# A chunked recurrence in front of two feed-forward layers: one triangular inverse for the first four chunks, and a new start

## The chip, the cores and the metric

The kernel runs on one core of a Trainium2 chip. The metric is the device time of one execution in microseconds (us); three runs of the kernel before gave 1090.04, 1091.82 and 1099.68 us, and their median, 1091.82 us, is the time before. The engines are TensorE (PE in the profile, with its weight loads as PEld), VectorE (DVE), ScalarE (ACT), GpSimd (POOL) and SyncE (SP, which only issues DMA transfers here).

## The reference

An attention-like recurrence over 768 steps for 4 batches of 8 heads with a state of 40 x 40, then two feed-forward layers over the 3072 tokens. All of it is float32.

```python
state = zeros((B, H, D, D))                       # B, H, S, D = 4, 8, 768, 40
for t in range(S):
    y[:, :, t] = einsum('bhd,bhde->bhe', rt, state)
    Sa = einsum('bhde,bhe->bhd', state, at)
    state = state * wt[:, :, None, :] - einsum('bhd,bhe->bhde', Sa, bt)
    state = state + einsum('bhd,bhe->bhde', vt, kt)
x = y.transpose(0, 2, 1, 3).reshape(3072, 320)
h = x @ w_in;   x = (h * tanh(log1p(exp(h)))) @ w_out      # 320 -> 2048 -> 320 (mish; h itself above 20)
h = x @ w_in2;  out = (h * cos(h)) @ w_out2
```

## The kernel before

**The recurrence** is cut in time into 24 chunks of 32 tokens and in batches into two halves of 16 heads, which gives 48 chunk steps, `g` = 0 to 47 (chunk `g // 2`, half `g % 2`). Every chunk step has work that doesn't need the state, `pre(g)` and `inverse`, and work that does, `chain(g)`.

`pre(g)` loads a, k, b and w (tile IN; for step 1 a part of TMP). VectorE scans the decays into PE (L570) and their inverse into RP (L575, L576), scales a into AM (L584, two passes) and k and b into KB (L590, two passes); GpSimd clears the other rows of AM (L598). TensorE multiplies AM by KB (L607, 8 matmuls), VectorE masks the product into AM (L617, four instructions of 64 partitions and 128 elements). Two DMAs store a triangular part to DRAM (`l_d`, L630, L631). TensorE transposes KB (L640), and ScalarE copies that into FL (L390).

`inverse(bt)` inverts the unit triangular 32 x 32 matrices of a batch of two chunk steps. They are read back into XM, one matrix half in a partition (L667, 64 partitions), 14 columns are worked off by a multiplication (L682, into XT) and an addition (L680), on VectorE for the batches 0 to 2 and on GpSimd for the others; the result goes to DRAM (`t_d`, L693) and back (TT, L697). `halves` joins the two halves with a transposition on VectorE and matmuls (L719, L721).

`chain(g)` runs from the state of step `g - 2`: right-hand sides (L790) to RS (L796), the multiplication by TT (L804, L813), copies into FR and VR, a product (L862) and its masked eviction (L872, 64 x 256), the matmul for the outputs and the new state (L888), evictions to SV (L899) and Y (L907), a transposition of the state (L932). After every second chunk Y is stored to `x_d`.

**The first layer** takes 256 tokens at a time (12 blocks). A block loads XR from `x_d` (L1042 to L1044), splits it into a high part XH (L1047) and a low part XL (L1049), and runs 8 rounds of matmuls (L991), Mish on ScalarE, GL on VectorE (L1067) and output matmuls (L972). Its weights come as pairs of 32-bit words and are converted in `prep`: load (L454), L461 on ScalarE, L466, L471 and L479 on VectorE, a high part (L390 or L392) and a low part on GpSimd (L508). The late half of w_out passes through two small buffers, RL. The second layer follows the same way and is not touched.

**The order on each engine** is fixed before the kernel runs. Every piece of work is a `Task` with an engine, a cost, predecessors, buffers (rings) and a priority; the class `Plan` goes through all tasks with these costs and writes one list for each engine, SP's transfers among them. Priorities come from a base and the step: -1e4 for `chain`, -5e3 for `pre`, -4921 for the weights, 0 and up for the layers. Lines that matter here:

```python
BATCH = [(i, 2) for i in range(0, TOT, 2)]
own = bt >= 3
ldma[g] = P.add("SP", 1.0, ldm, preds=t_gl, lat=DMA_LAT, prio=pr)
t_k = fifo("kb", P.add(*am_on(g, 0.65), kb_f(0), preds=[t_rp], acq=[("KB", k("KB"))], prio=pr, port=True))
t_b = P.add(*am_on(g, 0.65), kb_f(1), preds=[t_k, t_a1], ...)
```

Of the kernel before, what the change touches and what calls it, by code (L numbers as in the profile page):

```python
# [18 lines left out]
D = 40  # L19
# [69 lines left out]
SP_SAFE = 1.0  # L89

# [8 lines left out]
class Plan:  # L99
# [23 lines left out]
    def run(self):  # L123
# [12 lines left out]
        port_free = 0.0  # L136
# [4 lines left out]
        while done < len(self.tasks):  # L141
# [88 lines left out]
            t.end = free[e] + (0.2 if t.lat is None else t.lat)  # L230
# [6 lines left out]
            for u in t.succ:  # L237
                for x in u.engs:
                    u.ready[x] = max(u.ready[x], free[e] + (HOP.get((e, x), 0.15) if t.lat is None else t.lat))
# [12 lines left out]
def body(ctx, tc, ins, out):  # L252
# [11 lines left out]
    BATCH = [(i, 2) for i in range(0, TOT, 2)]  # L264
# [46 lines left out]
    P.ring("XR", 1), P.ring("XH", 2), P.ring("XL", 2), P.ring("OB", 2)  # L311

    D1 = at.tile([104, NQ, C + 1], F32, name="D1")
    IN_t = [at.tile([104, 3 * 256 + 265], F32, name=f"IN{i}") for i in range(N_IN)]
    IN1 = TMP[0:104, 4096:4096 + 1033]
# [20 lines left out]
    for n, k in (("IN", N_IN), ("PE", LA), ("AM", LA), ("FL", LA), ("RP", 1), ("KB", 1), ("SV", N_SV),  # L336
                 ("FR", N_FR), ("VR", N_VR), ("X", N_X), ("TT", N_TT), ("RS", 2), ("ZS", 1), ("Y", N_Y),
                 ("PA", 4), ("PH", 2), ("PO", 2)):
# [67 lines left out]
    DMA_LAT = 3.0  # L406
# [6 lines left out]
    AHEAD_W = 6  # L413
# [3 lines left out]
    am_on, GLE = lambda g, d: ("DVE", 0.385), ("DVE",)  # L417
# [4 lines left out]
    W1_AFTER = lambda: None  # L422
    W2_PRIO = 5e3
# [8 lines left out]
    def prep(layer, names, prio, after, stage, stage2, half):  # L432
# [7 lines left out]
        for (kind, k, cc), h, n in parts:  # L440
            late = kind == "out" and cc >= 5
            if late and t_sw is None:
# [12 lines left out]
                       preds=after + ([t_sw] if late else []) + loads[-AHEAD_W:][:1] * (len(loads) >= AHEAD_W),  # L455
                       acq=[(rring, (key, "r"))], lat=DMA_LAT + 1.5, prio=prio)
# [85 lines left out]
    Gev, KBe, scanT, ldma, ttld, tt_last, ytask = {}, {}, {}, {}, {}, {}, {}  # L542
    io, Sev, STev, chain_last = {}, {}, {}, {}
# [9 lines left out]
    def pre(g):  # L553
# [5 lines left out]
        pe, am, kb, rp = (lambda: PE_t[P.at(k("PE"))]), (lambda: AM_t[P.at(k("AM"))]), \  # L559
# [794 lines left out]
```

## Time and profile before

| what | value |
|---|---|
| runs of the kernel before | 1090.04, 1091.82, 1099.68 us |
| the profiled execution: its time, its span | 1096.53 us, 1094.8 us |
| instructions in the span | 36345 |
| busy over the span: TensorE, VectorE | 1011.0 us (92%), 746.4 us (68%) |
| busy over the span: ScalarE, GpSimd | 544.2 us (50%), 439.7 us (40%) |
| mean granted TensorE clock | 0.989 |

Busy time is the time in which an engine worked on an instruction. The span runs from the first to the last record of the profiled execution; its own time holds 1.7 us more. A busy share over the whole span says little here, because the first 130 us and the rest have different limits, and the views that matter are those of stretches.

### The profile page before, as it was taken

The numbers are of one execution on the slowest core, as the hardware profiler recorded it, in microseconds if no ns is written. First come the engines' busy times: TensorE is split into PE (matmuls) and PEld (weight loads), VectorE is DVE, ScalarE is ACT, GpSimd is POOL, SyncE is SP. The second block draws the span as 40 slices with busy tenths as digits, with TensorE's granted clock in tenths as the row PEclk, the third lists the DMA queues.
The fourth block names the chain that finished last, engine by engine and source line by source line (L and its number), as shares of the span: only waits on it lengthen the run. The fifth ranks groups of instructions, "written<-read, shape, count | busy, mean of one in ns | idle before, by whom it ended". The sixth has DMA issues, their size and how long they took to land.

```text
span 1094.8 us, 36345 instructions
## 1 busy us (share of the span) xinstructions
PE 1011.0 (92%) x14888; PEld 928.6 (85%) x14888; DVE 746.4 (68%) x1667; ACT 544.2 (50%) x1342; POOL 439.7 (40%) x885
## 2 busy tenths in 40 slices
PE   2266899899999999999999999999999999999998
PEld 1256798798988898988899989999999999999997
DVE  8999887768677677667743797446655556565555
ACT  3255666655565565655665544444433434343433
POOL 5215367553464655444730233103333333333332
PEclk9999899999999999989999999999999999999999
DMA  8555564646555565555543543211100202010100
GB/s 243 147 152 159 158 181 128 167 118 187 135 130 155 133 164 133 136 136 153 139 106 87 174 146 104 71 46 45 42 13 1 54 1 53 1 40 1 25 1 25
DMA packets 109366, 111.88 MB, mean 102 GB/s; under 512 B 64144, under 2 KB 88720, under 8 KB 109200
## 3 DMA queue, kind: packets, MB, share of 16 engines
q1 hardware_dynamic: 108880, 109.24, 36.6%
q8 instruction: 117, 1.92, 0.7%
q14 instruction: 49, 0.40, 0.1%
q10 hardware_dynamic: 320, 0.33, 0.1%
HBM read 91.43 MB, written 18.09 MB: 100 GB/s over the span
## 4 chain that ended last, share of the span: by engine, by line
PE 73%; DVE 11%; DMA 5%; issue 4%; POOL 3%; ACT 3%; SPq 1%; DVEq 0%; POOLq 0%; ACTq 0%
PE bank L991 16%; PE bank L972 15%; PE bank L1006 13%; PE bank L1022 13%; PE bank L888 4%; PE bank L862 2%; PE bank L836 2%; PE bank L607 2%; PE bank L640 1%; POOL XT L682 1%; PE bank L804 1%; DMA TT<-t_d 1%; DMA XM<-l_d 1%; PE bank L790 1%; PE bank L932 1%
## 5 line engine op out<-in xcount | busy, mean ns | idle before, releaser
L1150 POOL TENSOR_TENSOR GL<-H,GH 128x512 fp32r<-128x512 f32 x94 | 121.9, 1297 | 235.7 <-ACT GH L1148 219.1
L682 POOL TENSOR_TENSOR XT<-XM 64x14 f32<-64x14 f32 (+6 forms) x294 | 106.8, 363 | 180.8 <-DMA XM<-l_d 150.9
L390 ACT ACTIVATE FL<-bank 64x160 f32<-64x160 f32 (+1 forms) x376 | 101.5, 295 | 92.5 <-PE bank L932 45.4
L1141 ACT ACTIVATE T<-T,half_pi 128x512 f32<-128x512 f32 x96 | 69.4, 723 | 105.3 <-DVE T L1138 105.3
L1134 DVE TENSOR_SCALAR T<-bank 128x512 f32<-128x512 f32 x96 | 66.4, 692 | 76.6 <-PE bank L1006 63.0
L1067 DVE TENSOR_TENSOR GL<-H,GH 128x512 fp32r<-128x512 f32 x96 | 70.7, 739 | 69.7 <-ACT GH L1064 69.0
L680 POOL TENSOR_TENSOR XM<-XM,XT 64x14 f32<-64x14 f32 (+6 forms) x294 | 107.3, 365 | 22.5
L1062 ACT ACTIVATE H<-bank 128x512 f32<-128x512 f32 x96 | 57.5, 598 | 105.7 <-PE bank L991 105.0
L1143 DVE TENSOR_TENSOR H<-bank,T 128x512 f32<-128x512 f32 x96 | 66.1, 689 | 54.0 <-ACT T L1141 53.2
L1148 ACT ACTIVATE GH<-H 128x512 fp32r<-128x512 f32 x96 | 60.6, 632 | 73.9 <-DVE H L1143 72.7
L991 PE MATMUL bank<-XH,wih 128*128 128x256 f32 x448 | 94.9, 294 | 0.2 <-ACT GH L1064 0.2
L991 PE MATMUL bank<-XH,wil 128*128 128x256 f32 x448 | 90.0, 283 | 0.0
L991 PE MATMUL bank<-XL,wih 128*128 128x256 f32 x448 | 89.7, 282 | 0.0
L607 PE MATMUL bank<-AM,KB 104*64 104x64 f32 x768 | 37.3, 248 | 49.9 <-DVE KB L590 41.6
L617 DVE TENSOR_TENSOR AM<-bank,maskG 64x128 f32<-64x128 f32 x192 | 55.2, 287 | 34.8 <-PE bank L607 22.6
L607 PEld LDWEIGHTS bank<-AM,KB 104*64 104x64 f32 x768 | 30.9, 157 | 54.6 <-issue 38.6
L991 PEld LDWEIGHTS bank<-XH,wih 128*128 128x128 f32 x448 | 70.5, 193 | 2.2 <-ACT GH L1064 0.4
L991 PEld LDWEIGHTS bank<-XL,wih 128*128 128x128 f32 x448 | 69.7, 192 | 1.4 <-issue 1.4
L991 PEld LDWEIGHTS bank<-XH,wil 128*128 128x128 f32 x448 | 69.8, 193 | 0.0
L991 PE MATMUL bank<-XH,wix 128*128 128x256 f32 x224 | 67.8, 302 | 1.3 <-issue 1.3
L1138 DVE SCALAR_TENSOR_TENSOR T<-T,bank 128x512 f32<-128x512 f32 x96 | 65.7, 685 | 2.4
L888 PE MATMUL bank<-FR,FL 104*64 104x72 f32 x1536 | 62.9, 239 | 2.6 <-ACT wih L390 1.7
(173 smaller groups left out, 2933.4 us busy)
## 6 DMA issues: line engine op xcount, KB each, us to landing
VR<-in_vR_dram SPq DMA_DIRECT2D x96, 160.0 KB
IN<-in_inT_dram SPq DMA_DIRECT2D x94, 161.4 KB
FR<-in_rI_dram SPq DMA_DIRECT2D x48, 180.0 KB
FR<-in_vF_dram SPq DMA_DIRECT2D x48, 144.0 KB
TMP<-in_w_in_dram SPq DMA_DIRECT2D x12, 512.0 KB
RA<-in_w_in_dram SPq DMA_DIRECT2D x12, 512.0 KB
RA<-in_w_out_dram SPq DMA_DIRECT2D x10, 512.0 KB
SV<-in_vS_dram SPq DMA_DIRECT2D x96, 52.0 KB
```

What stands on the lines that cost most here:

```text
L390: A.activation(o, i, AF.Copy)
L607: PE.matmul(gp[c0:c0 + 64, q // 2], kb()[:, q].rearrange("p a t -> p (a t)"), am()[0:104, :, q], start=True, stop=True)
L680: IE.tensor_tensor(out=b[:, 0:i, i + 1:16], in0=b[:, 0:i, i + 1:16], in1=tv, op=ALU.add)
L682: IE.tensor_tensor(out=tv, in0=bc(b[:, i:i + 1, i + 1:16], (2 * n, i, w)), in1=bc(b[:, 0:i, i:i + 1], (2 * n, i, w)), op=ALU.mult)
L888: PE.matmul(fp[64 * p:64 * p + 64, qp], fl()[0:104, n * D:n * D + 64], fr()[:, n], start=True, stop=True)
L972: PE.matmul(o, l[:, f, tsl], r, start=(first and f == 0 and i == 0), stop=(last and f == 1 and i == 2))
L991: PE.matmul(hp[:, f], pss[i][0], pss[i][1], start=(i == 0), stop=(i == 7))
L1006: PE.matmul(bank[P.at((key, "h"))][:, 0:512], pss[i][0], pss[i][1], start=(i == 0), stop=(i == 7))
L1022: PE.matmul(o, l, r, start=(ft == 0 and i == 0), stop=(ft == NFF - 1 and i == 2))
L1067: gl = P.add(GLE, (dve(512),), lambda eng, Hv=Hv, key=key: EN[eng].tensor_tensor(out=GL_t[P.at((key, "gl"))], in0=Hv(), in1=GH_t[P.at((key ...
L1141: c = P.add("ACT", act(512, False, 1), lambda f=f, Tv=Tv: A.activation(Tv(f), Tv(f), AF.Sin, scale=-TWO_PI, bias=half_pi), preds=[b], aset ...
L1150: gl = P.add(*((VG, (pool(512), dve(512))) if final and quad == 7 else ("POOL", pool(512))), lambda eng, f=f, Hv=Hv, key=key: EN[eng].tens ...
```

## The change

- `BATCH` begins with one batch of four chunk steps (128 partitions of XM); the others keep two. VectorE inverts the batches 0 and 1 (`OWN`), that is the steps 0 to 5 as before, in two inversions where there were three.
- The transfers of batch 0 (`l_d`, XM, `t_d`, TT; `QUICK`) are issued on ScalarE's queue.
- k and b are scaled by one instruction (`kb_f`, 104 x 512).
- For the first 14 steps (`SPLIT`) the chunk product is 16 matmuls that read only the 40 rows in use; GpSimd clears nothing, and VectorE evicts in two instructions of 64 x 256.
- Clearing of SV, VR, `half_pi` and of the first states in FL goes from VectorE to GpSimd.
- The input tiles are cleared and loaded in the order 0, 2, 1, ahead of the weights; the weight loads are gated on input loads and on the load of TT. All eight PSUM banks serve the recurrence until XR of block 0 is loaded. Step 7 keeps its PE in an output buffer. For chunk 1, Y is evicted ahead of SV, and block 0's input gets a chain priority.
- `Plan` computes when a transfer lands from its size and a queue, no longer as a constant.

```diff
-    BATCH = [(i, 2) for i in range(0, TOT, 2)]
+    BATCH = [(0, 4)] + [(i, 2) for i in range(4, TOT, 2)]
...
     def setup_v():
         for t in SV_t:
-            V.memset(t, 0.0)
+            G.memset(t, 0.0)
         for t in VR_t:
-            V.memset(t[32:64], 0.0)
-        V.memset(half_pi, math.pi / 2)
+            G.memset(t[32:64], 0.0)
+        G.memset(half_pi, math.pi / 2)
...
+    OWN = 2
+    SPLIT = 14
+    QUICK = 4
+    AHEAD_W = 5
+    W1_FREE = 4
...
-                       preds=after + ([t_sw] if late else []) + loads[-AHEAD_W:][:1] * (len(loads) >= AHEAD_W),
-                       acq=[(rring, (key, "r"))], lat=DMA_LAT + 1.5, prio=prio)
+                       preds=(after if layer == 2 else [tt_ld[2]] if len(loads) >= W1_FREE else [t_in[2]]) + ([t_sw] if late else []) + (loads[-AHEAD_W:][:1] * (len(loads) >= AHEAD_W) if len(loads) >= W1_FREE else loads[-1:]),
+                       acq=[(rring, (key, "r"))], kb=0.5 * n, prio=prio)
...
-        def kb_f(j):
-            return lambda eng: EN[eng].tensor_tensor(out=kb()[:, :, j], in0=sl(1 + j), in1=rp()[:, :, 1:], op=ALU.mult)
+        def kb_f(eng):
+            EN[eng].tensor_tensor(
+                out=kb().rearrange("p q j t -> p j q t"), in0=INv()[:, 256:768].rearrange("p (j q t) -> p j q t", j=2, t=C),
+                in1=bc(rp()[:, :, 1:].unsqueeze(1), (104, 2, NQ, C)), op=ALU.mult)
...
+        split = g < SPLIT
+        if not split:
+            t_z0 = P.add("POOL", 0.31, az_f(0), preds=[t_a1], prio=pr)
+            t_z1 = P.add("POOL", 0.31, az_f(1), preds=[t_z0], prio=pr)
...
             for q in range(NQ):
+                if split:
+                    for p in range(2):
+                        r, o = slice(64 * p, 64 * p + 40), slice(64 - 64 * p, 128 - 64 * p)
+                        PE.matmul(gp[o, q], kb()[r, q].rearrange("p a t -> p (a t)"), am()[r, p, q], start=True, stop=True)
+                    continue
...
+                if split:
+                    V.tensor_tensor(out=am()[r, p], in0=pa(k("G"))[r, 0:256].rearrange("r (q t) -> r q t", t=C),
+                                    in1=bc(maskG[r].unsqueeze(1), (64, NQ, C)), op=ALU.mult)
+                    return
...
+        quick = g < QUICK
+        Q = A if quick else SP
         def ldm():
-            SP.dma_start(ld_v[ci, 0], am()[96:128, 0])
-            SP.dma_start(ld_v[ci, 1], am()[32:64, 1])
+            Q.dma_start(ld_v[ci, 0], am()[96:128, 0])
+            Q.dma_start(ld_v[ci, 1], am()[32:64, 1])
...
-        own = bt >= 3
+        own = bt >= OWN
...
+        early = c == 1
...
+            if early:
+                yevs.append(P.add("DVE", 0.26, yev(h), preds=[ft] + yevs, acq=y_acq, prio=pr - 30))
...
+        prx = -9.955e3 if blk == 0 else pr0
...
-            V.memset(FL_t[P.at(("FL", g))][64:104, 0:NU * D], 0.0)
+            G.memset(FL_t[P.at(("FL", g))][64:104, 0:NU * D], 0.0)
```

On ScalarE, at its very start, the queue of the kernel before begins with the weights' first pass (H from TMP) and its copies, and holds no transfer (FL0 is step 0's transposed KB, RS its right-hand sides).

```order
L461 ACT_TABLE_LOAD
L461 ACTIVATE H0_177<-TMP_172 128x512
L461 ACTIVATE H1_178<-TMP_172 128x512
L461 ACTIVATE H2_179<-TMP_172 128x512
L390 ACTIVATE wih1_164<-H0_177 128x512
L390 ACTIVATE wih1_164<-H1_178 128x512
L390 ACTIVATE wix1_166<-H2_179 64x512
L390 ACTIVATE GH0_180<-H2_179 64x512
L390 ACTIVATE FL0_208<-bank1_145 64x160 x4
```

In the changed kernel the same queue, from where step 3 has been transposed, holds the stores of `l_d`, the load of XM, the store of `t_d` and both loads of TT, with weights between them.

```order
L662 DMA l_d0_93<-AM3_202 32x8x32
L663 DMA l_d0_93<-AM3_202 32x8x32
L396 ACTIVATE FL3_209<-bank1_143 64x160 x4
L471 ACTIVATE H1_176<-TMP_170 128x512
L706 DMA XM_222<-l_d0_93 64x512 x2
L396 ACTIVATE wih1_162<-H1_176 128x512
L471 ACTIVATE H2_177<-TMP_170 128x512
L471 ACTIVATE H0_175<-TMP_170 128x512
L734 DMA t_d0_116<-XM_222 64x512 x2
L740 DMA TT0_229<-t_d0_116 128x8x32
L740 DMA TT1_230<-t_d0_116 128x8x32
```

Two weights' passes now stand in front of the store of `t_d`, and the weights' copies wait behind the transfers. On VectorE, in front of the first inversion, the kernel before evicts step 2 (AM2), works on weights and scales k and b of step 3 in two passes; the first inversion's first step is the last row.

```order
L584 TENSOR_TENSOR AM3_204<-IN0_192,PE3_197 40x256
L617 TENSOR_TENSOR AM2_203<-bank1_145,maskG_175 64x4x32 x4
L471 SCALAR_TENSOR_TENSOR H1_178<-TMP_172,H1_178 128x512
L590 TENSOR_TENSOR KB0_217<-IN0_192,RP0_215 104x8x32
L466 TENSOR_SCALAR H2_179<-H2_179 128x512
L590 TENSOR_TENSOR KB0_217<-IN0_192,RP0_215 104x8x32
L682 TENSOR_TENSOR XT_225<-XM_224 64x14
```

In the changed kernel it scales k and b of step 3 in one pass, evicts step 3 right behind it, and has seven instructions between that eviction and the first step, of 128 partitions.

```order
L605 TENSOR_TENSOR KB0_215<-IN0_190,RP0_213 104x2x8x32
L642 TENSOR_TENSOR AM3_202<-bank0_142,maskG_173 64x256 x2
L476 TENSOR_SCALAR H1_176<-H1_176 128x512
L481 SCALAR_TENSOR_TENSOR H1_176<-TMP_170,H1_176 128x512
L583 SCALAR_TENSOR_TENSOR PE4_196<-IN1_191,D1_189 104x264
L590 RECIPROCAL D1R_214<-PE4_196 104x8
L591 SCALAR_TENSOR_TENSOR RP0_213<-IN1_191,D1R_214 104x264
L599 TENSOR_TENSOR AM4_203<-IN1_191,PE4_196 40x256
L723 TENSOR_TENSOR XT_223<-XM_222 128x14
```

The eviction of step 3, its transfers and the inversion stand closer together, with a PE product and two DMA trips between. On TensorE, where block 1 of the first layer begins (XH1), the kernel before comes from block 0's matmuls, with one transposition of the chain (L836) just ahead.

```order
L991 MATMUL bank5_149<-XL0_187,wih1_164 128x256 x2
L991 MATMUL bank5_149<-XL0_187,wix1_166 128x256
L836 MATMUL bank1_145<-ident_173,ZS0_230 40x128 x4
L991 MATMUL bank4_148<-XH1_186,wih1_164 128x256 x2
L991 MATMUL bank4_148<-XH1_186,wil1_165 128x256 x2
```

In the changed kernel a state transposition (L984), the products L908 and L632 and `halves` (L764) stand just ahead of the same row; counted over the whole queue up to it, there are the products of twelve steps (L908) where there were eight (L862), the output and state matmuls and the state transpositions (L984) of eleven steps where there were eight (L888, L932), and the right-hand sides of twelve where there were ten (L790).

```order
L984 MATMUL bank2_144<-ident_171,SV0_216 104x40 x4
L984 MATMUL bank0_142<-ident_171,SV0_216 104x40 x4
L908 MATMUL bank6_148<-VR1_221 64x64 x8
L632 MATMUL bank3_145<-AM1_200,KB0_215 64x64 x8
L764 MATMUL bank2_144<-TA_224,TT0_229 32x32 x32
L1043 MATMUL bank4_146<-XH1_184,wih1_162 128x256 x2
```

More of the recurrence's work lies ahead of block 1 than before.

## Rows read from the trace of the kernel before

**Rows 1.** Windows: busy time (count) of PE, PEld, DVE, ACT, POOL; clock; DMA share; GB/s.

```profile
0.00:131.20 131.20, 67.73 (x1700) 56.84 (x1700) 120.22 (x331) 59.44 (x164) 47.36 (x107) 0.98 0.63 178
131.20:167.90 36.70, 36.49 (x562) 34.13 (x562) 31.15 (x84) 23.33 (x64) 22.92 (x53) 0.94 0.53 146
220.00:600.00 380.00, 370.79 (x8382) 335.92 (x8381) 259.27 (x692) 219.91 (x659) 180.18 (x522) 0.98 0.52 136
```

**Rows 2.** Waits of TensorE, 0 to 132 us: total us, times, longest.

```profile
PE bank L607 <- DVE KB L590: 41.6, 6, 16.9
```

**Rows 3.** Timeline of VectorE: start, us, line, operation; in brackets the idle time before.

```profile
16.39 0.42 DVE L590 TENSOR_TENSOR KB<-IN,RP 104x256 f32<-104x256 f32 x1
16.72 0.76 DVE L466 TENSOR_SCALAR H<-H 128x512 uint32<-128x512 uint32 x2
17.39 1.29 DVE L471 SCALAR_TENSOR_TENSOR H<-TMP,H 128x512 uint32<-128x512 uint32 x2
18.71 1.25 DVE L617 TENSOR_TENSOR AM<-bank,maskG 64x128 f32<-64x128 f32 x4
19.88 0.69 DVE L570 TENSOR_TENSOR_SCAN PE<-TMP,D 104x264 f32<-104x264 f32 x1
...
37.34 1.07 DVE L682 TENSOR_TENSOR XT<-XM 64x14 f32<-64x14 f32 x1 [0.28 <-DMA XM<-l_d]
...
130.24 0.96 DVE L1049 TENSOR_TENSOR XL<-XR,XH 128x768 fp32r<-128x768 f32 x1
...
166.91 0.95 DVE L1049 TENSOR_TENSOR XL<-XR,XH 128x768 fp32r<-128x768 f32 x1
```

**Rows 4.** Timeline of TensorE: the first matmuls of blocks 0 and 1.

```profile
132.45 0.80 PE L991 MATMUL bank<-XH,wih 128*128 128x256 f32 x2
...
174.03 0.48 PE L991 MATMUL bank<-XH,wih 128*128 128x256 f32 x2
```

**Rows 5.** VectorE by line and shape, 0 to 160 us: busy, mean ns | idle.

```profile
L617 DVE TENSOR_TENSOR AM<-bank,maskG 64x128 f32<-64x128 f32 x52 | 15.0, 288 | 2.8 <-PE bank L607 1.7
L872 DVE TENSOR_TENSOR FR<-bank,maskR 64x256 f32<-64x256 f32 x16 | 6.5, 418 | 1.4 <-PE bank L862 0.9 <-ACT FR L390 0.3
L355 DVE MEMSET VR<- 32x1024 f32 x2 | 1.8, 912 | 0.4 <-issue 0.4
L353 DVE MEMSET SV<- 128x832 f32 x2 | 1.5, 752 | 0.2
L682 DVE TENSOR_TENSOR XT<-XM 64x56 f32<-64x56 f32 x6 | 1.2, 204 | 0.1
L1206 DVE MEMSET FL<- 40x640 f32 x2 | 1.2, 592 | 0.4 <-issue 0.4
```

**Rows 6.** Timeline of GpSimd, its first weight pass.

```profile
17.29 4.36 POOL L508 TENSOR_TENSOR wil<-H,wih 128x512 fp32r<-128x512 f32 x2 [9.01 <-ACT wih L390]
```

**Rows 7.** The chain that ended last: start, us, what.

```profile
29.83 3.57 DMA l_d<-AM
...
87.37 2.10 DMA l_d<-AM
```

**Rows 8.** TensorE by line, 220 to 560 us: busy, mean ns | idle.

```profile
L888 PE MATMUL bank<-FR,FL 104*64 104x72 f32 x962 | 36.1, 229 | 0.1
L862 PE MATMUL bank<-VR 104*64 104x64 f32 x496 | 18.3, 225 | 0.0
L932 PE MATMUL bank<-ident,SV 40*104 40x40 f32 x240 | 16.4, 224 | 0.6 <-DVE Y L907 0.2
L790 PE MATMUL bank<-SV,AM 96*32 96x40 f32 (+1 forms) x960 | 13.1, 205 | 0.7 <-issue 0.4 <-DVE Y L907 0.3
```

**Rows 9.** Tile RL, all its instructions: ns min/median/max, first and last start.

```profile
L454 SPq DMA_DIRECT2D RL<-in_w_out_dram x10: 351/372/519, 124.1 to 179.2; - x10
...
L508 POOL TENSOR_TENSOR wol1b<-RL,woh1b x10: 716/733/2134, 145.4 to 189.8; 128x256 fp32r<-128x256 f32 x10
```

**Rows 10.** Windows, TensorE: busy time (count), clock, DMA share, GB/s.

```profile
125.00:130.00 5.00, 3.50 (x156) 0.54 0.85 212
```

More of the change, by code (lines that the diff above doesn't have):

```diff
@@ L135, in run @@
         done = 0
-        port_free = 0.0
+        port_free, queue = 0.0, 1.5
         recent = []
@@ L229, in run @@
                 port_free = free[e]
-            t.end = free[e] + (0.2 if t.lat is None else t.lat)
+            lat = t.lat
+            if t.kb:
+                queue = max(queue, free[e]) + t.kb / RATE
+                lat = queue + LAND - free[e]
+            t.end = free[e] + (0.2 if lat is None else lat)
             for key in t.rel:
@@ L621, in pre @@
         t_gl = []
-        for c2 in range(2):
+        for c2 in range(1 if split else 2):
             for p in range(2):
-                t_gl.append(P.add("DVE", 0.27, gev(p, c2), preds=[t_g], rel=[k("G")], prio=pr))
+                t_gl.append(P.add("DVE", 0.4 if split else 0.27, gev(p, c2), preds=[t_g], rel=[k("G")], prio=pr))
         Gev[g] = t_gl
@@ L657, in inverse @@
         n = cnt * NU
-        rows = lambda: slice(64 * P.at(("X", bt)), 64 * P.at(("X", bt)) + 2 * n)
+        slots = [("X", bt, i) for i in range((cnt + 1) // 2)]
+        r0 = lambda: 64 * min(P.at(i) for i in slots)
+        rows = lambda: slice(r0(), r0() + 2 * n)
         x = lambda: XM[rows(), 0:528]
@@ L915, in chain @@
         sevs, yevs = [], []
+        early = c == 1
         for h, ft in ((0, f0), (1, f1)):
             s = []
-            if not last:
+            rel = [k(f"F{h}")] + ([k("PE")] if h == 1 and g != PX else [])
+            y_acq = [("Y", ykey)] if (yc == 0 and h == 0) else []
+            if early:
+                yevs.append(P.add("DVE", 0.26, yev(h), preds=[ft] + yevs, acq=y_acq, prio=pr - 30))
+                for p in range(2):
+                    s.append(P.add("DVE", 0.315, sev(h, p), preds=[yevs[-1], io[nx][2]] + s, rel=rel if p else [], prio=pr))
+            elif not last:
                 s = [P.add("DVE", 0.315, sev(h, p), preds=[ft, io[nx][2]], prio=pr) for p in range(2)]
             sevs += s
-            rel = [k(f"F{h}")] + ([k("PE")] if h == 1 else [])
-            y_acq = [("Y", ykey)] if (yc == 0 and h == 0) else []
-            yevs.append(P.add("DVE", 0.26, yev(h), preds=[ft] + s + yevs, acq=y_acq, rel=rel, prio=pr + 1))
+            if not early:
+                yevs.append(P.add("DVE", 0.26, yev(h), preds=[ft] + s + yevs, acq=y_acq, rel=rel, prio=pr + 1))
         Sev[g] = sevs
@@ L1188, in body @@
     state_init = {}
+    for g in range(4):
+        pre(g)
+    inverse(0)
     for g in range(TOT):
+        if g > 3:
+            pre(g)
         load_step(g)
-        pre(g)
-        if BT_OF[g][1] == BATCH[BT_OF[g][0]][1] - 1:
+        if g > 3 and BT_OF[g][1] == BATCH[BT_OF[g][0]][1] - 1:
             inverse(BT_OF[g][0])
@@ L1233, in switch @@
             P.grow(r, range(len(STG[r])), P.time)
-        P.grow("PH", [0, 1], P.time)
-        P.grow("PO", [2, 3], P.time)
+        rest = sorted(i for _, i in P.rings["PA"])
+        P.grow("PH", rest[0:2], P.time)
+        P.grow("PO", rest[2:4], P.time)
     def half2():
```

122 lines of the change are left out of this document (70 added, 52 removed).

## The prediction

> **What bounds the kernel now.** I read the windows first [rows 1]. Up to 131.2 us VectorE works 120.22 us (91.6%) and TensorE 67.73. Then it turns: from 131.2 to 167.9 TensorE is busy 36.49 of 36.70 us, and between 220 and 600 us 370.79 of 380. So VectorE sets the end of the first stretch, and TensorE everything behind it. The waits say the same: of TensorE's idle time up to 132 us, 41.6 us end with the scaling of k and b on VectorE [rows 2]. From this follows how the change can pay: TensorE's work behind 132 us is fixed, and the end comes earlier by the work of TensorE that is done earlier, that is by the time at which VectorE lets it through. Two marks show this: the low part of block 0's input is written at 130.24 us and that of block 1 at 166.91 [rows 3], and their first matmuls run at 132.45 and 174.03 [rows 4].
>
> **Part by part**, for the stretch up to block 1's input, on VectorE.
>
> *Clearing.* Two VR at 0.912 us, two SV at 0.752 and two FL at 0.592 go to GpSimd [rows 5]: 4.5 us. GpSimd sat idle for 9.01 us ahead of its first weight pass at 17.29 [rows 6], so it costs nothing there. If the masks, which stand first, left no room, the first use of SV would wait at most the 4.5 us that were saved.
>
> *One inversion less.* 28 instructions at about 0.20 us (the 64x56 form of [rows 5], the largest): 5.6 us. The inversion that is left has 128 partitions where there were 64. Rows suggest that the time goes by the elements in a partition and not by the partitions: 256 elements take 0.42 us in 104 partitions (L590, [rows 3]) and 0.418 in 64 (L872, [rows 5]). So I take the price of a step as unchanged; the other bound, double, is a rival below.
>
> *Chunk products.* Four evictions of 0.288 us become two of 64x256, for which L872 with the same shape has 0.418 [rows 5]: 1.15 to 0.84, or 0.31 us a step, for 14 steps 4.4 us. On TensorE 16 matmuls with 40 rows take the place of 8; it waits in this stretch, and I put it at nothing. GpSimd's clearing of AM goes off the path from AM to the product.
>
> *One pass for k and b.* Two passes of 0.42 us [rows 3] for 256 elements; the row of 768 elements has 0.96, and between the two 512 elements come to 0.69. That is 0.15 us a step, over some 16 steps 2.3 us. Its bounds are 0 (as long as two passes) and 0.42 a step, that is 6.7.
>
> Together 4.5 + 5.6 + 4.4 + 2.3 = 16.8 us.
>
> *What it adds.* In the order of the changed kernel the eviction of step 3 stands right behind the scaling of the same step. In the kernel before, with the same path through TensorE, the scaling that starts at 16.39 ends at 16.81, and two weights' passes fill the time until the eviction at 18.71 [rows 3]: now 1.9 us of this is idle. Behind the eviction, the trip of step 3's matrix goes out to DRAM and back. Before, the store was issued at 29.83 us [rows 7], and the first step began at 37.34 [rows 3]: 7.5 us. In the new order stand between them two weights' passes (0.38 and 0.65), two scans (0.69 each), one pass of AM (0.42, as another of 256 elements) [rows 3] and a short reciprocal, together 3.1 us. The uncovered wait is at most 7.5 - 3.1 = 4.4 us; with both trips at 2.10, the other price of such a store [rows 7], it is 4.7 - 3.1 = 1.6 (0.5 for the two gaps). I take 3.3, nearer to the upper end, since the trip belongs to the same crowded start as the one at 29.83. Behind the waiting step stand all of VectorE's later steps, and ScalarE's conversion of weights behind its own transfers. Some 0.5 us come from the first input, which now waits for nothing but its own landing. Together 5.7 us, so 16.8 - 5.7 = 11.1 us are left.
>
> The Trainium skill, page "DMA: Bandwidth & Descriptors", section "Issuing engines are not separate DMA queues", speaks against the move to ScalarE's queue: transfers of all issuing engines share the same 16 DMA engines and interleave, so that only issue time is saved. By this rule the two trips would stay at 3.57 instead of 2.10 us, which is 2.9 us later, the upper end of the wait; the sum would be 10.0 in place of 11.1.
>
> *A second count, from the orders.* Up to block 1's input VectorE's list has 381 instructions where there were 414; priced with the rows of before they are 1.3 us more, because steps of the chain take the place of what was saved. TensorE's list at block 1's first matmul is ahead: four products L862 at 0.59 us, three of the outputs and states L888 at 1.20, three transpositions L932 at 0.55 and two right-hand sides L790 at 0.44 (busy time of [rows 8], divided by the 31, 30, 30 and 30 steps in them): 2.4 + 3.6 + 1.7 + 0.9 = 8.6 us. One chunk product, two multiplications by TT, two transpositions of those and three joins of halves come on top, seven or eight things between 0.44 and 0.69, an estimate from the same rows: 3.1 to 5.5. So 11.7 to 14.1 us of TensorE's work lie ahead of block 1 at about the same time, and 1.3 go off: 10.4 to 12.8, if VectorE's waits stay as long as they were (11.0 us up to 131.2 and 5.6 in the next stretch [rows 1]). One of these is gone: the second chunk step had to wait for a second inversion, and its matrix now comes with the first. For that I add 1 to 2 us. Both counts meet at about 13 us, and the forecast is 1091.8 - 13 = 1079 us. The profiled execution took 1096.53 us for a span of 1094.8, 4.7 more than the median, so the profile of the changed kernel should have a span between 1077 and 1082. Block 0's first matmul should come at about 103 us, since VectorE has 28.8 us less to do ahead of it (233 instructions for 331); this is no gain by itself, as work is only put behind it.
>
> **The rivals.** About 1% (11 us) is what a measurement of this kernel can tell from no change.
>
> *Given back by the late weights.* In the kernel before, the late half of w_out is loaded from 124.1 us and its last low part starts at 189.8 [rows 9], 66 us later. In the new order of SP these loads stand behind the stores of step 13 and of the fourth inversion, and VectorE's list up to the eviction of step 13, priced with the rows of before, ends at about 131. If block 0 starts 29 us earlier, its last output matmuls want these weights 29 us earlier, and TensorE, whose order is fixed, stands still: with the old spacing the last part comes at about 198. Of the 13 us forecast, 8 to 13 would be lost and 0 to 5 be left: 1087 to 1092. Against it: block 0 has six rounds ahead of them, and the new order leaves more of the chain between. Chance 0.22.
>
> *Larger.* The 16.6 us of gaps in VectorE's first 168 us [rows 1] close, since the chain has its inverse early and all eight banks. Then block 1 starts 11 to 13 us earlier and the work ahead counts as well: 24 to 26 us, 1066 to 1068. TensorE's own work from 103 us to there is about 61 us, which is just what fits. Chance 0.14.
>
> *It doesn't do what it says:* the inversion of 128 partitions costs twice that of 64, 5.6 us more. Half of the gain is gone: 1085. Chance 0.07.
>
> *Slower, by the clock.* The granted clock was 0.54 between 125 and 130 us, where TensorE had been busy with pieces of the chain, against 0.98 over the first stretch [rows 1, 10]; 0.5 of the scale is 1.2 GHz, 1.0 is 2.4. From 103 to 174 us it must do some 61 us of full-speed work in 71. What runs at the lower level takes twice as long, so that beyond 10 us of such work each further us is lost. If 34 of the 61 us ran there, 24 us would be lost and 11 would remain as a loss: 1103. Against it: with matmuls of the first layer the next stretch read 0.94 [rows 1]. Chance 0.07, which has its turning point at 23 us of work at the lower level.
>
> **How the numbers follow.** The forecast has 0.50; its own range is 1071 to 1086, from the bounds of the single pass (up to 4.4 us more gain), of the trip (1.1 less, 1.7 more) and of the second count. Faster by over 1% means under 1081: four fifths of the forecast's half, whose own range reaches further down than up (0.40), and all of the larger case (0.14): 0.54. Slower has the clock's 0.07, the rest is 0.39. The range leaves out the slow case, the lower fringe of the larger one and the top of the late weights: 1063 to 1090.
>
> **What would show it.** Right: VectorE's clearing is gone from its first microseconds; evictions of chunk products of 64x256 at about 0.42 us, the single pass at 0.6 to 0.75, steps of 128 partitions at 0.20; the first inversion's step begins with idle time of 2 to 4 us on the DMA of XM; block 0's first matmul near 103 us and block 1's near 172 with 12 us more of the chain in front. Wrong: TensorE idle on the high or low parts of the late w_out between 140 and 200 us; a clock of half between 103 and 170; a block 1 that starts by 165, which would be the larger case; or an idle TensorE between 220 and 600 us, where nothing should have changed.

## The result, and the profile after

The changed kernel takes 1104.28 us (median of 20 runs, 1095.36 to 1113.52) against 1091.58 for the kernel before (20 runs). The ratio is 1.0104, with a 95% interval of 1.0085 to 1.0123: it is 1% slower, where 1079 us was forecast. The run of 1113.52 us had a lower mean granted clock (0.963, the others 0.981 to 0.990) and isn't counted in the ratio. Its profiled execution has a span of 1102.2 us.

The windows of the changed kernel, with the columns of [rows 1]: its first 40 us, then up to the first matmul of block 0, then up to the first matmul of block 1.

```profile
0.00:40.00 40.00, 12.93 (x208) 11.07 (x208) 27.00 (x60) 7.53 (x22) 13.66 (x46) 1.00 0.46 125
...
0.00:117.80 117.80, 66.43 (x1548) 58.44 (x1548) 92.31 (x235) 50.23 (x140) 34.68 (x72) 1.00 0.62 178
117.80:200.40 82.60, 74.49 (x1586) 66.62 (x1584) 61.12 (x148) 50.24 (x143) 49.84 (x119) 0.90 0.53 146
```

The first 40 us of the kernel before, in the same columns:

```profile
0.00:40.00 40.00, 10.44 (x144) 8.14 (x144) 35.64 (x89) 14.28 (x33) 17.54 (x52) 1.00 0.72 214
```

VectorE's idle time in the first 40 us is 13.0 us where it was 4.4, ScalarE works half as long, and the DMA engines move 125 GB/s in place of 214. Up to block 0 VectorE is idle for 25.5 us of 117.8; before it was 11.0 of 131.2 [rows 1]. VectorE's work up to block 1 is 92.31 + 61.12 = 153.4 us, 2.0 more than the 120.22 + 31.15 = 151.4 of the kernel before [rows 1]; the orders priced with the rows of before gave 1.3 more. The prices were right, and the waits were not.

The timeline of VectorE in the changed kernel around the first inversion shows them:

```profile
27.51 0.68 DVE L605 TENSOR_TENSOR KB<-IN,RP 104x512 f32<-104x512 f32 x1
30.21 0.88 DVE L642 TENSOR_TENSOR AM<-bank,maskG 64x256 f32<-64x256 f32 x2 [2.02 <-PE bank L629]
35.79 0.43 DVE L476 TENSOR_SCALAR H<-H 128x512 uint32<-128x512 uint32 x1 [4.70 <-ACT H L471]
36.25 0.69 DVE L481 SCALAR_TENSOR_TENSOR H<-TMP,H 128x512 uint32<-128x512 uint32 x1
39.26 1.15 DVE L583 TENSOR_TENSOR_SCAN PE<-IN,D 104x264 f32<-104x264 f32 x1 [2.32 <-DMA IN<-in_inT_dram]
...
42.58 0.17 DVE L723 TENSOR_TENSOR XT<-XM 128x14 f32<-128x14 f32 x1 [0.88 <-DMA XM<-l_d]
```

The single pass (0.68), the evictions (0.88 for two) and the steps of 128 partitions (0.17 to 0.22) cost what was forecast. Between the eviction and the first step stand six instructions, not the seven of the text above. The two passes that were to cover the trip of the matrix wait 4.70 us for a weight, the scan behind them 2.32 us for an input, and the first step 0.88 us for XM: 7.9 us of idle time, where 3.3 were forecast. All of it lies inside the trip, as ScalarE's timeline shows:

```profile
30.67 0.33 ACTq L662 DMA_DIRECT2D l_d<-AM  x1
31.12 0.38 ACTq L663 DMA_DIRECT2D l_d<-AM  x1
...
36.67 1.16 ACTq L706 DMA_DIRECT2D XM<-l_d  x2
```

From the second store to the first step, at 42.58, are 11.5 us, where the forecast had 7.5 at most. SP's load behind the first of these stores (L576, in the list of waits below) is issued at 36.27, when that store has landed, and XM is loaded right behind. By these times the two passes would have been done sooner with their weights there, and the first step would have waited for XM all the same.

When the weights come is seen by their tiles. In the changed kernel TMP (the early ones) and RL (the late half of w_out) read:

```profile
L471 ACT ACTIVATE H<-TMP x17: 646/658/682, 18.3 to 133.4; 128x512 f32<-128x512 f32 x17
...
L464 SPq DMA_DIRECT2D RL<-in_w_out_dram x10: 352/386/1362, 154.2 to 200.4; - x10
...
L518 POOL TENSOR_TENSOR wol1b<-RL,woh1b x10: 729/1002/2899, 166.9 to 209.3; 128x256 fp32r<-128x256 f32 x10
```

In the kernel before the first passes over TMP started between 5.3 and 117.2 us, and RL ran from 124.1 to 189.8 [rows 9]. Everything of the weights is later by 13 to 30 us, though block 0 begins earlier. TensorE's timeline in the changed kernel shows what comes of that:

```profile
117.83 0.79 PE L1043 MATMUL bank<-XH,wih 128*128 128x256 f32 x2
118.42 0.63 PE L1043 MATMUL bank<-XH,wil 128*128 128x256 f32 x2
...
137.53 1.92 PE L629 MATMUL bank<-AM,KB 40*64 40x32 f32 x32 [5.59 <-ACT GH L396]
...
140.60 0.63 PE L1043 MATMUL bank<-XH,wil 128*128 128x256 f32 x2
...
153.10 0.40 PE L1043 MATMUL bank<-XH,wil 128*128 128x256 f32 x2
...
200.45 0.50 PE L1043 MATMUL bank<-XH,wih 128*128 128x256 f32 x2
```

Block 0 starts at 117.83 us (before 132.45 [rows 4]), and block 1 at 200.45 (before 174.03). The same pair of matmuls takes 0.63 us at 118 and 0.40 at 153, and 5.59 us go by idle ahead of a chunk product. The view puts this wait down to the copy of a weight (GH, L396), which ended just then. But the product reads AM and KB, and in the program it waits for the scaling of k and b; on VectorE that ran until 137.38:

```profile
136.69 0.69 DVE L605 TENSOR_TENSOR KB<-IN,RP 104x512 f32<-104x512 f32 x1
```

VectorE had been busy since 131.54, with four passes over late weights (2.2 us) among its work.

How much TensorE loses can be summed up. I priced each of its matmuls at the time it has where rows run at full speed (a pair of L1043 0.40 us, 32 of L629 1.12, 64 of L934 2.22, and so on) and took the sum of these prices from the time of the stretch: what is left is idle time and slowness. In us, by stretches of the execution profiled:

| kernel | 0 to 117 | 117 to 200 | 200 to 600 |
|---|---|---|---|
| before | 84.5 | 12.2 | 34.7 |
| changed | 81.0 | 23.6 | 27.5 |

From 117 to 200 us the change loses 11.4 us more. The windows of that stretch, TensorE alone (columns as in [rows 10]), in the kernel before, the changed kernel and e3 below:

```profile
117.00:200.00 83.00, 77.73 (x1618) 0.94 0.56 152
```

```profile
117.00:200.00 83.00, 74.89 (x1565) 0.90 0.53 145
```

```profile
117.00:200.00 83.00, 78.48 (x1704) 0.94 0.58 159
```

So 2.8 of the 11.4 us are idle time, and the rest is slowness. The split adds 6 us of full-speed work to the first 200 us (14 steps of 0.43). In the other stretches the change loses 10.7 less. That makes 6.7 us, and the spans of the two profiled executions differ by 7.4; the medians differ by 12.7, since the profiled execution of the kernel before took 5 us more than its median. A few records are missing from traces, so each sum is good to some 3 us.

### The profile page after: what moved, and what is told of

Same layout as the page of the kernel before. It is cut to its first block, busy times and chain, and to the rows that moved or that the text cites. A ratio compares the mean times of both kernels' runs of the same rounds, so it can differ in the third digit from the quotient of the medians.

```text
span 1102.2 us, 36623 instructions
## 1 busy us (share of the span) xinstructions
PE 1026.5 (93%) x15112; PEld 944.9 (86%) x15112; DVE 727.5 (66%) x1553; ACT 544.4 (49%) x1344; POOL 428.4 (39%) x864
## 4 chain that ended last, share of the span: by engine, by line
PE 76%; DVE 3%; issue 2%; ACT 1%; DMA 1%; SPq 0%; DVEq 0%; ACTq 0%
PE bank L1024 17%; PE bank L1043 16%; PE bank L1058 13%; PE bank L1074 13%; PE bank L934 3%; PE bank L632 2%; PE bank L908 2%; PE bank L882 2%; PE bank L984 1%; PE bank L673 1%; PE bank L836 1%; PE bank L850 1%; PE bank L766 1%; PE bank L764 1%; PE bank L1168 1%
## 5 line engine op out<-in xcount | busy, mean ns | idle before, releaser
L723 POOL TENSOR_TENSOR XT<-XM 64x14 f32<-64x14 f32 (+6 forms) x294 | 99.4, 338 | 177.8 <-DMA XM<-l_d 156.3
L396 ACT ACTIVATE FL<-bank 64x160 f32<-64x160 f32 (+1 forms) x376 | 101.8, 296 | 113.1 <-PE bank L673 54.2
L721 POOL TENSOR_TENSOR XM<-XM,XT 64x14 f32<-64x14 f32 (+6 forms) x294 | 104.6, 356 | 22.9
L1119 ACT ACTIVATE H<-bank 128x512 f32<-128x512 f32 x96 | 57.4, 598 | 113.3 <-PE bank L1043 112.3
L1043 PE MATMUL bank<-XH,wih 128*128 128x256 f32 x448 | 95.8, 296 | 0.0
L1043 PE MATMUL bank<-XH,wil 128*128 128x256 f32 x448 | 89.7, 282 | 0.0
L1043 PE MATMUL bank<-XL,wih 128*128 128x256 f32 x448 | 89.5, 282 | 0.0
L918 DVE TENSOR_TENSOR FR<-bank,maskR 64x256 f32<-64x256 f32 x96 | 38.9, 419 | 53.9 <-PE bank L908 20.6
L1043 PEld LDWEIGHTS bank<-XH,wih 128*128 128x128 f32 x448 | 70.0, 191 | 2.5
L1043 PEld LDWEIGHTS bank<-XL,wih 128*128 128x128 f32 x448 | 69.6, 192 | 0.0
L1043 PEld LDWEIGHTS bank<-XH,wil 128*128 128x128 f32 x448 | 69.4, 191 | 0.0
L1043 PE MATMUL bank<-XH,wix 128*128 128x256 f32 x224 | 67.5, 301 | 0.0
L629 PE MATMUL bank<-AM,KB 40*64 40x32 f32 x448 | 24.5, 277 | 44.2 <-DVE KB L605 38.6
L934 PE MATMUL bank<-FR,FL 104*64 104x72 f32 x1536 | 65.1, 245 | 0.2
L1024 PE MATMUL bank<-woh1a,GH 128*128 128x320 f32 x192 | 65.1, 339 | 0.0
```

The source lines that it names most:

```text
L396: A.activation(o, i, AF.Copy)
L721: IE.tensor_tensor(out=b[:, 0:i, i + 1:16], in0=b[:, 0:i, i + 1:16], in1=tv, op=ALU.add)
L723: IE.tensor_tensor(out=tv, in0=bc(b[:, i:i + 1, i + 1:16], (2 * n, i, w)), in1=bc(b[:, 0:i, i:i + 1], (2 * n, i, w)), op=ALU.mult)
L934: PE.matmul(fp[64 * p:64 * p + 64, qp], fl()[0:104, n * D:n * D + 64], fr()[:, n], start=True, stop=True)
L1024: PE.matmul(o, l[:, f, tsl], r, start=(first and f == 0 and i == 0), stop=(last and f == 1 and i == 2))
L1043: PE.matmul(hp[:, f], pss[i][0], pss[i][1], start=(i == 0), stop=(i == 7))
```

## The experiments

Four theories were tried. A: ScalarE's stores make SP stand still. B: the gate on the weight loads holds the weights back. C: the split products cost TensorE's time. D: the order is a draw, which any edit throws anew, as small differences in the planned durations decide what stands first. The later expectations call it F that each part has its own price. The runs of the kernel before that go with an experiment gave medians of 1091.5 to 1092.7 us. A point, below, is one hundredth of the time of the kernel before, 10.9 us. All results in one table:

| kernel | median us | ratio to before, 95% interval |
|---|---|---|
| changed | 1104.28 | 1.0104 (1.0085 to 1.0123) |
| e1: batch 0 on SP's queue | 1094.98 | 1.0043 (1.0010 to 1.0076) |
| e2: no split | 1098.96 | 1.0064 (1.0033 to 1.0094) |
| e3: weight gate undone | 1085.46 | 0.9955 (0.9930 to 0.9981) |
| e4: other draw | 1101.56 | 1.0099 (1.0065 to 1.0133) |
| e5: e3, no split | 1090.44 | 0.9971 (0.9945 to 0.9996) |
| e6: e3, SP's queue | 1081.63 | 0.9903 (0.9872 to 0.9934) |
| e7: half of the gate undone | 1090.46 | 0.9992 (0.9969 to 1.0015) |
| e8: e3, batches of two | 1102.27 | 1.0091 (1.0060 to 1.0122) |
| e9: before, other draw | 1094.92 | 1.0031 (0.9997 to 1.0065) |
| e10: e6, other draw | 1086.93 | 0.9950 (0.9924 to 0.9976) |
| e11: before, the gate alone | 1111.06 | 1.0165 (1.0111 to 1.0218) |
| e12: before, clearing and one pass | 1096.73 | 1.0041 (1.0012 to 1.0070) |
| e13: e6, no split | 1079.15 | 0.9887 (0.9847 to 0.9926) |
| e14: e6, clearing and two passes on VectorE | 1082.29 | 0.9906 (0.9876 to 0.9936) |
| e15: e6, batches of two | 1088.84 | 0.9977 (0.9950 to 1.0004) |

**The gate (e3, e7, e11).** e3 gives the weight loads the conditions of the kernel before:

```diff
-    AHEAD_W = 5
+    AHEAD_W = 6
-  preds=(after if layer == 2 else [tt_ld[2]] if len(loads) >= W1_FREE else [t_in[2]]) + ([t_sw] if late else [])
-        + (loads[-AHEAD_W:][:1] * (len(loads) >= AHEAD_W) if len(loads) >= W1_FREE else loads[-1:]),
+  preds=after + ([t_sw] if late else []) + loads[-AHEAD_W:][:1] * (len(loads) >= AHEAD_W),
```

> The changed kernel with the weight loads of the first layer gated as before (no wait for the input loads and for TT, six loads ahead). Theory B: the first pass of the last early weight comes near 121 us instead of 133.4, TensorE's wait of 5.6 us at 132 us and a part of the slow clock go, 1094 to 1098 us. Theory A: weights come earlier and inputs later, SP's waits on l_d stay at 12 us and more, within 4 us of the changed kernel. Theory C: no change. Theory D: anything between 1090 and 1110.

It came out at 1085.46 us, under theory B's range. The windows of e3, its first 40 us, and its tile TMP:

```profile
0.00:40.00 40.00, 12.59 (x208) 10.90 (x208) 35.61 (x69) 14.41 (x33) 18.57 (x50) 1.00 0.62 181
```

```profile
L471 ACT ACTIVATE H<-TMP x17: 653/662/689, 4.8 to 99.1; 128x512 f32<-128x512 f32 x17
```

VectorE's idle time in the first 40 us is back at 4.4 us, the last early weight starts at 99.1 instead of 133.4, and block 1 at 168.5. TensorE's loss between 117 and 200 us, counted as above, is 13.6 us instead of 23.6. These are 10.0 of the 18.7 us between the two profiled spans (1102.2 and 1083.5); the others lie outside that stretch, and no view here says what they are. The trip of the matrix is not shorter: the first step of the inversion begins at 46.21, later than with the gate. e7 takes the wait for TT away alone:

```diff
-  [tt_ld[2]] if len(loads) >= W1_FREE else [t_in[2]]
+  [t_in[2]] if len(loads) >= W1_FREE else [t_in[2]]
```

> The changed kernel with one half of the gate undone: weight loads from the fifth on wait for the input load of step 2 as the first four do, no longer for TT. Theory F: the wait for TT holds most of the weights back, VectorE's idle time in the first 40 us falls from 13.0 to under 7 us, and the time comes near the kernel without a gate, 1085 to 1092. If the first half of the gate and the five loads ahead cost it, 1099 to 1104.

It came out at 1090.46 us, within the first range. By the ratios this is 1.12 of the 1.49 points that e3 gained. But VectorE's first 40 us changed little:

```profile
0.00:40.00 40.00, 12.96 (x208) 11.07 (x208) 28.41 (x62) 9.99 (x27) 13.35 (x46) 1.00 0.53 152
```

So the expected cause, filling work in the first 40 us, isn't what brought this gain: VectorE is idle for 11.6 us, not under 7. What e3 and e7 have in common is that the bulk of the weights no longer waits for the inversion: in e7 the last early weight starts at 110.5 us (133.4 with the gate, 99.1 in e3), and RL at 133.7 (154.2). The other direction is e11, which puts the gate into the kernel before, with `t_in` and `tt_ld` recorded there:

```diff
-    AHEAD_W = 6
+    AHEAD_W = 5
+    W1_FREE = 4
-  preds=after + ([t_sw] if late else []) + loads[-AHEAD_W:][:1] * (len(loads) >= AHEAD_W),
+  preds=(after if layer == 2 else [tt_ld[2]] if len(loads) >= W1_FREE else [t_in[2]]) + ...
```

> The kernel before with the weight gate of the change alone (the first four loads wait for the input of step 2 and for one another, the later ones for TT of the second inversion). Theory F: VectorE and ScalarE lose the weights as filling work at the start, block 0 waits for them, TensorE's first 200 us hold 10 us more of idle and slow time: 1103 to 1115. If the gate hurts only with the other parts of the change: 1089 to 1095.

1111.06 us, as the theory had it. Windows and tile TMP of e11:

```profile
0.00:40.00 40.00, 7.98 (x124) 6.36 (x124) 31.78 (x96) 6.67 (x18) 8.98 (x47) 1.00 0.48 133
```

```profile
L462 ACT ACTIVATE H<-TMP x17: 652/660/699, 31.7 to 143.3; 128x512 f32<-128x512 f32 x17
```

The gate costs 1.65 points alone and 1.49 with the rest of the change: 16 to 18 us, more than the whole loss of 11. Both e3 and e11 change the number of loads ahead (`AHEAD_W`) together with the gate.

**The queue (e1, e6).** `QUICK = 4` becomes `QUICK = 0`, in the changed kernel and in e3.

> The changed kernel with the transfers of batch 0 back on SP's queue (QUICK 0), all else as changed. Theory A: in the changed kernel SP stands still behind ScalarE's stores of l_d (16.2 us of waits up to 40 us), inputs and weights come late, and TensorE gets its work too thinly from 118 to 200 us. Then SP's waits on l_d fall under 5 us, VectorE's idle time ahead of block 0 falls from 25.5 us to about 15, block 0's first matmul comes near 108 us instead of 117.8, and the time is 1093 to 1098 us. Theory B (the gate on the weight loads holds the weights back, whatever the queue): within 3 us of the changed kernel, 1101 to 1107. Theory C (the split products cost TensorE's time): no change, 1101 to 1107. Theory D (the list of each engine is a draw, which any edit throws anew): anything between 1090 and 1110, and block 1's first matmul moves without SP's waits being the reason.

> The kernel with the weight gate undone (1085.5 us), and the transfers of batch 0 on SP's queue besides (QUICK 0). Theory A (SP stands still behind ScalarE's stores): SP's waits on l_d (10.7 us up to 118 us) go, inputs come earlier, 1080 to 1083. Theory F (the queue is of little account once there is other work for VectorE): 1084 to 1088. If ScalarE's queue helps at all, the first step of the inversion comes later than with it, by 1 to 4 us, and the time is 1086 to 1090.

What theory A is about is in the list of waits of SP's queue, in the changed kernel up to 60 us:

```profile
SPq L792 <- DMA l_d<-AM: 7.7, 2, 4.6
SPq L576 <- DMA l_d<-AM: 4.7, 1, 4.7
SPq L798 <- DMA l_d<-AM: 3.8, 1, 3.8
```

Loads of VR, IN and SV, which read nothing of `l_d`, are issued only when ScalarE's stores of `l_d` have landed. With SP's queue these waits are gone (16.2 us in the changed kernel, 10.7 in e3). Both runs are faster, by 0.61 and 0.52 points (1.0104 to 1.0043, 0.9955 to 0.9903), and their times lie in theory A's ranges. Yet the place isn't the one forecast: in e1 block 0 begins at 117.68 and block 1 at 199.66, as in the changed kernel, and the loss up to 200 us is the same (105.3 against 104.6); what it gains lies behind 320 us. In e6 the weights do come sooner, as its tiles TMP and RL show, and block 0 doesn't (116.2, in e3 112.3):

```profile
L471 ACT ACTIVATE H<-TMP x17: 647/660/713, 4.8 to 80.3; 128x512 f32<-128x512 f32 x17
...
L518 POOL TENSOR_TENSOR wol1b<-RL,woh1b x10: 716/736/1504, 119.0 to 176.4; 128x256 fp32r<-128x256 f32 x10
```

The first inversion itself begins at 41.34 in e1 (42.58 in the changed kernel) and at 50.77 in e6 (46.21 in e3), once sooner and once later without ScalarE's queue. The queue brings no time, and seems to cost 6 us, not much more than the largest draw below; that it does so by SP's waits isn't shown.

**The draw (e4, e9, e10).** `TIE = 97` becomes 98, in the changed kernel, in the kernel before and in e6.

> The changed kernel with one constant of the planner changed (TIE 97 to 98), which alters each planned duration by at most 1% and nothing else. Theory D: the time moves by more than 5 us, because the order is a draw. Theories A, B and C: the time stays within 4 us of the changed kernel's 1104, with SP's waits on l_d and TensorE's thin stretch in it as before.

> The kernel before with one constant of the planner changed (TIE 97 to 98). Theory F (each part has a price of its own): within 5 us of 1091.6, 1087 to 1097. Theory D (the order is a draw and that of the kernel before was a good one): 1097 to 1110.

> The kernel with the weight gate undone and batch 0 on SP's queue (1081.6 us), with the same constant changed (TIE 97 to 98). Theory F: 1079 to 1087. Theory D: 1088 to 1100.

The times lie in the ranges of theories A to C (e4) and F (e9, e10). The ratio moves by -0.05, +0.31 and +0.47 points. An edit's effect of under half a point can be the order's and not the edit's. The gate's 1.5, seen in two kernels, is three times the largest of these three draws.

**The split (e2, e5, e13).** `SPLIT = 14` becomes 0, in the changed kernel, in e3 and in e6.

> The changed kernel with the chunk products of all steps as before (SPLIT 0: 8 matmuls, AM cleared by GpSimd, four evictions). Theory C: TensorE's busy time for these products falls from 47.5 us to about 37, of which the 5 or 6 steps behind 118 us count: 3 to 5 us less, 1099 to 1101, though VectorE's evictions take 4 us more. Theories A and B: no gain, 1103 to 1108, since VectorE has more to do. Theory D: anything between 1090 and 1110.

> The kernel with the weight gate undone (1085.5 us), and the chunk products of all steps as before (SPLIT 0) besides. Theory F (each part has its own price: the gate holds VectorE idle in the first 40 us, the split costs TensorE 0.43 us at full clock in each of 14 steps and gains VectorE 4 us in a stretch where VectorE sets the time): TensorE's work falls by 6 us, VectorE's rises by 4, and the time is 1081 to 1086. Theory D (draw): anything from 1078 to 1095, with the gain or loss in stretches behind 320 us.

> The kernel with the weight gate undone and batch 0 on SP's queue (1081.6 us), and the chunk products as before (SPLIT 0). If the split's saving on VectorE (4 us) is worth its 6 us of TensorE's work: slower, 1084 to 1090. If VectorE's saving is lost in waits and TensorE's work counts: faster, 1075 to 1080. A draw: within 5 us either way, with TensorE's lost time behind 320 us as the difference.

Without it the ratio moves by -0.40, +0.16 and -0.16 points: no effect beyond a draw, though e5 came out 4 us over theory F's range. The lines of TensorE for the products, in the changed kernel:

```profile
L629 PE MATMUL bank<-AM,KB 40*64 40x32 f32 x448 | 24.5, 277 | 44.2 <-DVE KB L605 38.6 <-ACT GH L396 5.6
L632 PE MATMUL bank<-AM,KB 104*64 104x64 f32 x544 | 23.0, 227 | 1.4 <-DVE KB L605 0.7 <-POOL XT L723 0.6
```

and in e13, where all products are of the old kind:

```profile
L632 PE MATMUL bank<-AM,KB 104*64 104x64 f32 x768 | 37.3, 248 | 52.2 <-DVE KB L605 51.6 <-ACT RS L842 0.5
```

47.5 us against 37.3. A step has 32 records of 1.12 us together at full speed in place of 16 of 0.69. Ten of the fourteen split products run before 117 us, where TensorE waits anyway, which is why 10 us needn't show in the time.

**VectorE's savings (e12, e14).** e12 puts clearing and the single pass into the kernel before; e14 takes them out of e6.

```diff
-            V.memset(t, 0.0)                       # SV, VR, half_pi, FL: as in the change
+            G.memset(t, 0.0)
-        t_k = fifo("kb", P.add(*am_on(g, 0.65), kb_f(0), preds=[t_rp], ...))
-        t_b = P.add(*am_on(g, 0.65), kb_f(1), preds=[t_k, t_a1], ...)
+        t_b = fifo("kb", P.add("DVE", 0.6, kb_f, preds=[t_rp, t_a1], ...))
```

> The kernel before with two parts of the change alone: clearing on GpSimd (4.5 us) and one pass for k and b (some 4 us up to block 1, at 0.67 us a pass). Theory F: VectorE, which sets the time up to block 1, has 7 us less to do: 1083 to 1088. Theory D: anything between 1080 and 1100.

> The same 1081.6 us kernel, with clearing back on VectorE and k and b in two passes. If the saved work sets the time: 6 to 8 us slower, 1087 to 1090, and block 0's first matmul comes that much later than 116 us. If VectorE only waits more: within 4 us, 1078 to 1086.

In the kernel before, saving these 7 us makes it slower by 0.41 points, no more than a draw, where 4 to 9 us of gain were expected; in e6 giving them back costs 0.03. The windows up to 112 us of e6 and of e14:

```profile
0.00:112.00 112.00, 59.85 (x1465) 52.78 (x1466) 96.86 (x234) 50.32 (x136) 46.79 (x90) 1.00 0.64 180
```

```profile
0.00:112.00 112.00, 61.03 (x1490) 53.58 (x1492) 99.48 (x261) 52.95 (x146) 41.92 (x84) 1.00 0.65 188
```

VectorE works more in e14, and TensorE has done as much by then: the saved time seems to have become waiting (e6: 3.9 us for inputs alone, e14: none in its list). Block 0 starts at 116.2 and 117.1.

**The batch of four (e8, e15).** Batches of two and three inversions on VectorE, in e3 and in e6:

```diff
-    BATCH = [(0, 4)] + [(i, 2) for i in range(4, TOT, 2)]
+    BATCH = [(i, 2) for i in range(0, TOT, 2)]
-    OWN = 2
+    OWN = 3
     inverse(0)
+    inverse(1)
```

> The kernel with the weight gate undone (1085.5 us), and batches of two chunk steps throughout, three of them inverted on VectorE as before. Theory F: VectorE does 28 more steps of the inversion (5.6 us) ahead of block 1, block 0's first matmul comes 3 to 6 us later than with four (112 us), 1088 to 1093. If the larger batch only moves the first chain step back, no change or a gain: 1082 to 1086.

> The same 1081.6 us kernel, with batches of two chunk steps throughout and three of them inverted on VectorE. If the batch of four is what makes the gain: 1092 and more, as it was with ScalarE's queue (1102). If that was the ScalarE queue's or a draw's doing: 1082 to 1088, about the 5.6 us of one inversion at most.

Slower by 1.36 and 0.74 points, 8 to 15 us: e8 beyond its range, e15 between its two. Block 0 starts sooner without the batch of four (102.4 and 108.6 us), and block 1 much later (211.8 and 194.8). The chain's second step then has to wait for a second inversion again, which may be the reason; no run parts it from the 28 more instructions on VectorE. This is the one part whose removal made both kernels slower by more than the largest draw.

## Why the prediction was wrong

Its first step, that VectorE sets the end of the first stretch, holds as a description of before and fails as a rule for gains. The busy share of 91.6% is not a bound by throughput: inputs, trips and weights arrive in an order, and VectorE's freed time turned into waits (25.5 us instead of 11.0 up to block 0; saving the work moved the time by +0.41 points in e12 and, read from e14, by -0.03).

The step that failed by the most is "Together 5.7 us, so 16.8 - 5.7 = 11.1 us are left". It looked for new waits around the inversion alone, and the sum priced the weight gate at nothing. The order fences showed two weights' passes as the cover of the trip; that these weights are themselves gated, I read in the diff and didn't cost. The gate is worth 16 to 18 us, by e3 and e11, of the 25 between forecast and result. Without it the change gains 5 us (e3) where 13 were forecast. The wait at the trip was mis-sized as well, 7.9 us for 3.3, since the trip took 11.5 us and not 7.5; but this isn't what makes the kernel slower, for in e3 the first step comes 3.6 us later still.

"Block 0's first matmul should come at about 103 us, since VectorE has 28.8 us less to do" came out at 117.8. VectorE had 27.9 us less work up to it (120.22 and 92.31) and 14.5 us more waiting, and of the 29 us forecast 14.6 were left. In "11.7 to 14.1 us of TensorE's work lie ahead of block 1 at about the same time" the work was right, by the order, and "about the same time" was off by 26 us.

"On TensorE 16 matmuls with 40 rows take the place of 8; it waits in this stretch, and I put it at nothing" was mis-sized: 0.43 us a step at full speed, 10 us of busy time over the kernel. In the time it isn't visible beyond the draw.

The unit prices were right: the single pass 0.66 to 0.68 us against 0.69, the eviction 0.44 against 0.42, the step 0.17 to 0.22 against 0.20 (so the third rival, a double price for 128 partitions, is out), and VectorE's work of 153.4 us, 2.0 more than before against 1.3.

Of the rivals, the late weights named the right object with too small a price and too late a cause: RL began at 154.2 us where I had 131, and the early weights were late too. The slower clock named the right symptom. Between 117 and 200 us TensorE spent 29.5 us at the lower level in the changed kernel (up to 129.3, from 136.1 to 143.0, and from 187.3 to 197.6), 11.9 in the kernel before and 10.3 in e3. The fall at 136.1 lies in the gap of 5.59 us ahead of 137.53. With the gate undone and nothing else, the time at the lower level is back to that of before, so it goes along with the gate and needs no cause of its own. The 0.98 that this rival compares with is no reading for most of the first stretch, as the last section shows.

On ScalarE's queue, the rule of the Trainium skill, page "DMA: Bandwidth & Descriptors", section "Issuing engines are not separate DMA queues", that only issue time is saved, was the better guide: in both pairs the kernel was no slower without that queue (0.61 and 0.52 points faster).

What stays open is by what path the gate's 16 to 18 us arise outside 117 to 200 us, why e1 gains behind 320 us, and how much of the batch's 8 to 15 us is the order's. Some parts were never undone alone: the order of the inputs, the eight banks, Y ahead of SV, block 0's priority and the landing times in `Plan`. The diff also has conditions on transfers that neither the list of the change nor the sum names: an input load waits for the one before it, and the loads of FR, VR and SV for those of two steps earlier. The best version, e13 (no gate, SP's queue, no split, the rest of the change), takes 1079.15 us, 0.9887 (0.9847 to 0.9926) of the kernel before; it beats both. That it and e6 come near the 1079 us of the forecast doesn't confirm the sum, which had 6.8 us from clearing and the single pass; these gave nothing in e12 and e14.

## What to carry to other kernels

A busy share of 90% doesn't mean that work taken off the engine is time gained: look for what it would wait for next, in the same stretch, and cost every new condition on a transfer, not only the transfers that the change is about. Where weights are converted in the gaps of a dependent chain, a gate on their loads takes away the filling and delays what needs them; here it cost more than all the rest of the change brought. Where a planner orders the work, throw its draw once or twice before reading an effect of half a percent.

## What the runs showed of the hardware

Transfers issued on one engine's queue held up another's. In the changed kernel SP's loads of VR, IN and SV waited 16.2 us up to 60 us for ScalarE's stores of `l_d`, to which they have no data in common. The program's list of waits names the reason for the first of them. In ScalarE's and in SP's list, the store of step 0's `l_d` and the load of VR read:

```
L662 DMA l_d0_93<-AM0_199 32x8x32 [waits DMAHW2_49,DVE_49]
L792 DMA VR0_220<-in_vR_dram 40x1024 [waits DMAHW2_49,Pool_49]
```

In this program eight counters of completed transfers (DMAHW0 to DMAHW7) serve both queues, and a transfer waits for the one that used its counter before, whichever queue that was on. The trace agrees: the store is issued at 17.01 us on ScalarE's queue, and the load, on SP's, at 20.06.

A granted clock of 1.00 was not always a reading. In the trace of the changed kernel the first record of the clock begins at 129.3 us, and for the time ahead of it the windows print 1.00. Windows of TensorE cut at the records (columns as in [rows 10]):

```profile
117.00:129.30 12.30, 12.30 (x159) 1.00 0.36 104
129.30:136.10 6.80, 2.64 (x45) 1.00 0.48 118
136.10:143.00 6.90, 5.47 (x49) 0.51 0.24 61
143.00:187.30 44.30, 42.60 (x1106) 1.00 0.58 160
187.30:197.60 10.30, 9.48 (x160) 0.50 0.71 199
```

Where there are records, the pace of the matmuls goes with them: the pair of L1043 takes 0.63 us at 140.60, in the window of 0.51 (the lower level, 1.2 GHz), and 0.40 at 153.10, at 1.00 (2.4 GHz). Ahead of the first record it takes 0.63 us too, so TensorE ran at the lower level there. The same holds for the kernel before, whose first record begins at 118.6 us; its chunk product takes 1.12 us before it and 0.63 behind it:

```profile
64.49 1.12 PE L607 MATMUL bank<-AM,KB 104*64 104x64 f32 x16 [0.86 <-DVE KB L590]
...
118.72 0.63 PE L607 MATMUL bank<-AM,KB 104*64 104x64 f32 x16
```

Up to the first record the durations of repeated forms are the surer reading.
